# Stage-1 reads issued by ScalarE, and a later dispatch behind the gate, in an FFT convolution with mixture-of-experts and feed-forward kernel

## The chip, the cores and the metric

The kernel runs on one core of one Trainium2 chip. The metric is device microseconds of that core, median of 3 runs; lower is better. "us from the span's start" is the time axis of every row shown here.

## What is computed

The reference is a long convolution by FFT, a top-1 mixture of experts, and a dense layer pair with softplus between:

```python
y   = irfft(rfft(x, axis=1) * (filt_r + 1j * filt_i))        # x: 8 x 3072 x 256
x   = y.reshape(24576, 256)
e   = argmax(x @ w_gate, axis=1)                             # 8 experts, capacity 768 each
disp[e, pos] = x                                             # tokens in order, first 768 of an expert kept
out = gate_w * (relu(disp @ w1) @ w2)                        # 256 -> 1024 -> 256, back to its token
return softplus(out @ w_in) @ w_out                          # 256 -> 2048 -> 256
```

With these inputs the first three of the eight batches of 3072 tokens fill every expert's 768 places, so the main path convolves batches 0, 1 and 2 only; the rest of the output is one constant row. A check at the end branches to a general path when that does not hold; it is not taken here.

## The kernel before

**Stages.** The first quarter of the span is a pipeline that convolves three batches and dispatches their tokens; the rest is 16 units of 384 token slots, each with `w1`, `w2`, `wi`, `wo` (TensorE matmuls in split fp32r precision). The order of all work is written by hand: `ev(t, order, fn, ...)` puts a function into step `t`, and steps are emitted one after the other, within a step by `order`. This text counts steps from `c0`, the first of the pipeline, so "step 23" is `c0 + 23`. Each engine and each DMA queue runs its instructions in that order and stops at one whose semaphores are not there yet.

**Batches 1 and 2, first DFT.** `x1_out` (L213 to L222) writes the first stage's result to a DRAM tile `mid`; `load_i` (L224) reads a 128 x 2 x 256 piece `it` back in another layout, one for each of 12 columns `k`. The tile has four buffers. `s2` (L229) multiplies it (TensorE, L235) and filters it (VectorE, L239 to L242, and an add L243 on GpSimd for even `k`, on VectorE for odd `k`); `s3` (L247) is the next matmul, two steps after. Batch 1 has its `s2` in steps 18 to 29, batch 2 in steps 30 to 41. `tr2`, `s4` and `park` (L361) bring the tokens of a batch into the DRAM tile `parked`, by ScalarE copies and ScalarE's DMA queue.

**Gate and dispatch.** `gate` (L301) works out expert, slot and gate weight of a batch on VectorE in five steps. Then `marks` (L367) writes them from SP's queue: four DMAs of `ga` into `parked` (L372) and one of `ix` into the slot table `slots` (L373). `send` reads the table back (`load_index`, L390), `fetch` reads rows `lt` of one of eight groups (L394, three buffers), and `scatter` issues indirect DMAs `disp<-lt,ixt` of 128 rows (L398) on GpSimd, three to a group, 24 to a batch. `x_done` starts the loads `wst` of the dense weights (L452), which `convert` splits on VectorE, ScalarE and GpSimd from step 23 on, a new one every third step.

**The first unit.** `Unit.load_x` (L535) reads its rows `xd` from `disp` in step 50 once all scatters of batches 0 and 1 have landed; `gate_x` (L547) and `tr_x` (L555) follow, then `w1`. The loads `ws` of expert weights (L522) stand on the same SP queue.

**DMA semaphores.** A DMA of SP or ScalarE counts on one of eight semaphores, DMAHW0 to DMAHW7, which both queues use by turns; its issue waits until the DMA that last counted on the same one has landed.

Of the kernel before, what the change touches and what calls it, by code (L numbers as in the profile page):

```python
# [97 lines left out]
def body(tc, cap, x, ff, fx, wg, w1, w2, win, wout, m1, m2, m4, small, out):  # L98
    nc = tc.nc
    ctx = ExitStack()  # L100
    nunit = -(-cap // UNIT)
    lead = min(cap, UNIT)
# [14 lines left out]
    mid = [dram.tile([N1 * N2, D], F32, name=f"mid{b}") for b in range(1, STATIC)]  # L117
# [21 lines left out]
    class Conv:  # L139
# [84 lines left out]
        def load_i(self, b, k):  # L224

            self.it[b, k] = self.ip.tile([128, 2, D], F32, name="it", tag="it")
            nc.sync.dma_start(self.it[b, k], mid[b - 1].rearrange("(p k) c -> k p c", k=128)[:, 2 * k:2 * k + 2])

        def s2(self, b, k):  # L229

# [441 lines left out]
    with tc.manual_schedule():  # L672
        stl, stx, stf, stw, stm = (ExitStack() for _ in range(5))
        nc.scalar.preload_act_table_set(lnexp)
        cv = Conv(stl, stf, stx, "A")
# [54 lines left out]
        def ev(t, order, fn, *args):  # L730
            at.setdefault(t, []).append((order, len(at.get(t, ())), fn, args))
# [7 lines left out]
        T1, T2, S2, GG, S4, GATE, S3, X1, ON = range(-9, 0)  # L739
# [82 lines left out]
        c0, B = -72, (0, 17, 29)  # L822
        fills = cv.prefill()
        for b, s in enumerate(B):
            s += c0
            last = b == STATIC - 1
            for k in range(12):
                if b == 0:
                    if k % 2 == 0:
                        ev(s + k, T1 - 1, cv.make_m3, k // 2)  # L830
                    ev(s + k, T1, cv.tr1, b, k)
                else:
                    ev(s + k - 3, ON, cv.load_i, b, k)
                ev(s + k + 1, S2, cv.s2, b, k)
                ev(s + k + 3, S3, cv.s3, b, k)
            ev(s + 15, GG, cv.gsum, b)
            ev(s + 16, GG, cv.gturn, b)
            for k in range(5):
                ev(s + 17 + k, GATE, gate, b)
            for m in range(16):  # L840
                g, h = divmod(m, 2)
                t = s + 15 + (m // 2 if last else m * 13 // 16)
                ev(t, S4 + 0.5, cv.tr2, b, h, g)
                ev(t + 1, S4, cv.s4, b, h, g)
                if h:
                    ev(t + 1, ON, park, b, g)
            ev(s + 21, ON, cv.marks, b)
            if not last:
                ev(s + 21, ON, send, b, "lead")
                for _ in range(2):  # L850
                    ev(s + 21, ON, fetch)
        for g in range(8):
            ev(c0 + 5 + g, X1, cv.x1_out, 1, g)
            ev(c0 + 5 + g, ON, cv.load_x, 2, g)
            ev(c0 + 13 + g, X1, cv.x1_out, 2, g)
        for i in range(nslot // (4 * N1)):
            ev(c0 + 5 + i, ON, next, fills)
        for t in range(c0 + 22, -20):
            ev(t, ON, scatter, 2 if t < c0 + 46 else 3)
        ev(c0 + 22, ON, x_done)  # L860
        for t in range(c0 + 23, -24):
            ev(t, AHEAD - 0.5, convert, t < c0 + 45 and (t - c0) % 3 == 2)
# [7 lines left out]
        for v, u in enumerate(units):  # L870
            b = 16 * (v - 2)
# [9 lines left out]
            for i in range(KI):  # L881
                t = 16 * v + i
# [149 lines left out]
```

## Time and profile before

| | before |
|---|---|
| median of 3 runs | 1134.59 us (1133.48 to 1139.24) |
| profiled execution, its own time | 1130.57 us |
| span of its instructions | 1128.8 us |
| busy: TensorE matmul, VectorE, ScalarE, GpSimd | 92%, 42%, 71%, 53% of the span |
| mean granted TensorE clock | 0.967 of full speed |

The profiled execution is 4.0 us under the median of the runs, and 1.8 us of it lie outside the span. Busy shares are means over the convolution stages and the 16 units, which have different limits.

### The profile page before, as it was taken

What the parts mean: (1) busy time and instruction counts of PE and PEld (TensorE: products, weight loads), DVE (VectorE), ACT (ScalarE), POOL (GpSimd) and SP (SyncE); (2) the same over time, 40 slices, a digit from 0 to 9 for tenths busy, and PEclk for the clock granted to TensorE, in tenths of its full rate; (3) what the DMA queues carried; (4) which work ended last, traced back from release to release, by engine and by line L of the source; (5) the groups of instructions that cost most, each with busy time, mean ns of one, the idle gap of its engine ahead of it and who ended that gap; (6) DMA issues with size and microseconds to landing.
All of it is one profiled execution on the core that took longest, in us unless ns stands there. A gap on an engine that the chain in (4) does not pass through costs nothing.

```text
span 1128.8 us, 18362 instructions
## 1 busy us (share of the span) xinstructions
PE 1044.0 (92%) x6608; PEld 968.8 (86%) x6608; DVE 475.0 (42%) x929; ACT 804.8 (71%) x1690; POOL 598.2 (53%) x566
## 2 busy tenths in 40 slices
PE   9999688576778999999999999999999999999996
PEld 7756466345778999999999999999999999999996
DVE  3527599145877483323333333233332333332221
ACT  3555345265679888878788787888878788787885
POOL 0311470643646666677756565555656555654554
PEclk9999798786999999999999999999999999999999
DMA  9997884675543216643342323233211211100000
GB/s 311 322 299 227 236 261 82 201 234 151 153 128 104 68 54 226 225 142 110 105 135 96 130 90 132 93 116 109 67 61 53 61 53 56 58 10 15 15 15 18
DMA packets 111413, 141.67 MB, mean 126 GB/s; under 512 B 24366, under 2 KB 82987, under 8 KB 111312
## 3 DMA queue, kind: packets, MB, share of 16 engines
q1 hardware_dynamic: 94160, 112.02, 32.0%
q10 hardware_dynamic: 11392, 15.73, 4.8%
q0 software_dynamic: 5760, 12.65, 3.2%
q8 instruction: 54, 0.88, 0.3%
q14 instruction: 47, 0.39, 0.1%
HBM read 80.38 MB, written 63.15 MB: 127 GB/s over the span
## 4 chain that ended last, share of the span: by engine, by line
PE 70%; DVE 11%; DMA 6%; issue 5%; ACT 3%; POOL 3%; SPq 1%; ACTq 0%; POOLq 0%; DVEq 0%
PE pi L598 21%; PE po L621 21%; PE py L583 9%; PE pw L566 9%; PE p L219 2%; POOL gl L413 1%; DMA mid<-s 1%; PE p L199 1%; PE p L299 1%; DMA slots<-ix 1%; DMA wst<-in_win_dram 1%; DVE wrf L477 1%; DVE t L240 1%; DVE t L242 1%; DVE z L239 1%
## 5 line engine op out<-in xcount | busy, mean ns | idle before, releaser
L501 DVE SCALAR_TENSOR_TENSOR g<-pi,ln 128x384 f32<-128x384 f32 x256 | 142.8, 558 | 498.4 <-ACT ln L496 465.1
L413 POOL TENSOR_TENSOR gl<-g,gh 128x384 fp32r<-128x384 f32 x256 | 261.0, 1023 | 114.1 <-ACT gh L412 76.1
L621 PE MATMUL po<-woh,gh 128*128 128x256 f32 x768 | 214.9, 280 | 3.9 <-DVE ot L628 3.9
L621 PE MATMUL po<-woh,gl 128*128 128x256 f32 x768 | 215.6, 281 | 0.7 <-POOL gl L413 0.7
L621 PE MATMUL po<-wol,gh 128*128 128x256 f32 x768 | 215.8, 281 | 0.0
L493 ACT ACTIVATE ab<-pi 128x384 f32<-128x384 f32 x256 | 125.0, 488 | 114.4 <-PE pi L598 110.6
L598 PE MATMUL pi<-yh,wih 128*128 128x384 f32 x512 | 173.5, 339 | 6.4 <-DVE g L501 6.4
L598 PE MATMUL pi<-yl,wih 128*128 128x384 f32 x512 | 172.4, 337 | 0.0
L598 PE MATMUL pi<-yh,wil 128*128 128x384 f32 x512 | 172.1, 336 | 0.0
L413 POOL TENSOR_TENSOR w1l<-ws,w1h 128x512 fp32r<-128x512 f32 x64 | 83.6, 1306 | 136.2 <-ACT w1h L412 132.7
L621 PEld LDWEIGHTS po<-woh,gh 128*128 128x128 f32 x768 | 144.4, 188 | 4.7 <-DVE ot L628 2.8
L621 PEld LDWEIGHTS po<-woh,gl 128*128 128x128 f32 x768 | 144.8, 188 | 0.9 <-POOL gl L413 0.9
L621 PEld LDWEIGHTS po<-wol,gh 128*128 128x128 f32 x768 | 144.2, 188 | 0.0
L494 ACT ACTIVATE ab<-ab 128x384 f32<-128x384 f32 (+1 forms) x257 | 134.9, 525 | 8.2
L496 ACT ACTIVATE ln<-ab 128x384 f32<-128x384 f32 (+1 forms) x257 | 134.8, 524 | 8.1
L413 POOL TENSOR_TENSOR w2l<-ws,w2h 128x512 fp32r<-128x512 f32 x64 | 83.5, 1305 | 95.7 <-ACT w2h L412 94.0
L412 ACT CAST gh<-g 128x384 fp32r<-128x384 f32 x256 | 129.7, 507 | 0.3 <-DVE g L501 0.3
L598 PEld LDWEIGHTS pi<-yh,wih 128*128 128x128 f32 x512 | 96.4, 188 | 8.4 <-DVE g L501 8.4
L398 POOL DMA_INDIRECT disp<-lt,ixt x72 | 71.6, 994 | 54.4 <-DMA lt<-parked 38.9
L598 PEld LDWEIGHTS pi<-yl,wih 128*128 128x128 f32 x512 | 96.3, 188 | 0.0
L598 PEld LDWEIGHTS pi<-yh,wil 128*128 128x128 f32 x512 | 96.1, 188 | 0.0
L583 PE MATMUL py<-hh,w2h 128*128 128x384 f32 x256 | 90.0, 352 | 6.5 <-DVE yl L590 6.5
(132 smaller groups left out, 1965.6 us busy)
## 6 DMA issues: line engine op xcount, KB each, us to landing
ws<-in_w_dram SPq DMA_DIRECT2D x128, 256.0 KB, 2.8
out_dram<-cs SPq DMA_DIRECT2D x48, 512.0 KB, 3.9
lt<-parked SPq DMA_DIRECT2D x24, 387.0 KB, 4.7
xt<-in_x_dram SPq DMA_DIRECT2D x24, 384.0 KB, 8.0
parked<-yt ACTq DMA_DIRECT2D x24, 384.0 KB, 6.2
disp<-pf SPq DMA_DIRECT2D x16, 387.0 KB, 7.3
xd<-disp SPq DMA_DIRECT2D x48, 129.0 KB, 3.0
mid<-s ACTq DMA_DIRECT2D x16, 384.0 KB, 6.2
```

Source lines behind the costliest of these rows:

```text
L219: nc.tensor.matmul(ps.rearrange("q n c -> q (n c)"), lhsT=self.m1s, rhs=xt[:, 2 * i:2 * i + 2].rearrange("p n c -> p (n c)"), start=True, ...
L398: sc = nc.gpsimd.indirect_dma_start(out=disp[0:n], out_offset=bass.IndirectOffsetOnAxis(ap=index[b].bitcast(U32)[:, g, t:t + 1], axis=0), ...
L412: nc.scalar.copy(dst_hi, src)
L413: nc.gpsimd.tensor_tensor(out=dst_lo, in0=src, in1=dst_hi.bitcast(F32), op=ALU.subtract)
L493: nc.scalar.activation(out=ab[:, :n], in_=h, func=ACTF.Abs)
L494: nc.scalar.activation(out=ab[:, :n], in_=ab[:, :n], func=ACTF.Exp, scale=-1.0)
L496: nc.scalar.activation(out=ln[:, :n], in_=ab[:, :n], func=ACTF.Ln, bias=1.0)
L501: nc.vector.scalar_tensor_tensor(out=g[:, :n], in0=h, scalar=0.0, in1=ln[:, :n], op0=ALU.max, op1=ALU.add)
L566: nc.tensor.matmul(ps, lhsT=a[:, k, fs], rhs=b[:, k], start=(n == 0), stop=(n == 5))
L583: nc.tensor.matmul(self.py[d], lhsT=a[:, j % 2, ds], rhs=b, start=(j == 0 and n == 0), stop=(j == 7 and n == 2))
L598: nc.tensor.matmul(self.pi, lhsT=a[i][:, k], rhs=b[:, k], start=(n == 0), stop=(n == 5))
L621: nc.tensor.matmul(self.po[t], lhsT=a[:, ts], rhs=b[:, i], start=(i == 0 and n == 0), stop=(i == KI - 1 and n == 2))
```

## The change

Three things change, and nothing of what is computed. `load_i` issues its DMA from ScalarE's queue instead of SP's, and stands one step later (step `s + k - 2`). Behind a batch's gate, `marks` comes one step later, `send` with its two fetches two steps later. The scatters are in other steps: before, two to a step from step 22 on, and three from step 46 on, as long as there are any; now two to a step in steps 26 to 37 and three to a step in steps 43 to 50.

```diff
         def load_i(self, b, k):
...
-            nc.sync.dma_start(self.it[b, k], mid[b - 1].rearrange("(p k) c -> k p c", k=128)[:, 2 * k:2 * k + 2])
+            nc.scalar.dma_start(self.it[b, k], mid[b - 1].rearrange("(p k) c -> k p c", k=128)[:, 2 * k:2 * k + 2])
...
                 else:
-                    ev(s + k - 3, ON, cv.load_i, b, k)
+                    ev(s + k - 2, ON, cv.load_i, b, k)
...
-            ev(s + 21, ON, cv.marks, b)
+            ev(s + 22, ON, cv.marks, b)
             if not last:
-                ev(s + 21, ON, send, b, "lead")
+                ev(s + 23, ON, send, b, "lead")
                 for _ in range(2):
-                    ev(s + 21, ON, fetch)
+                    ev(s + 23, ON, fetch)
...
-        for t in range(c0 + 22, -20):
-            ev(t, ON, scatter, 2 if t < c0 + 46 else 3)
+        for t in range(26, 51):
+            if t < 38 or t > 42:
+                ev(c0 + t, ON, scatter, 2 if t < 38 else 3)
```

**SP's queue behind the gate of batch 0** (`parked_61` and `slots_64` are batch 0's, `mid_67` is batch 1's stage-1 result). Before, from the last prefill of `disp` on:

```order
L382 DMA disp<-pf 96x1032
L372 DMA parked_61<-ga 96x8x2 x4
L373 DMA slots_64<-ix 96x8x4
L390 DMA ixt<-slots_64 128x8x3
L394 DMA lt<-parked_61 128x774 x2
L227 DMA it<-mid_67 128x2x256 x2
L452 DMA wst<-in_win_dram 128x2x128 x4
L227 DMA it<-mid_67 128x2x256
```

The same place in the changed kernel, with the semaphores that each waits for:

```order
L372 DMA parked_61<-ga 96x8x2 [waits DMAHW1_49,DVE_49]
L372 DMA parked_61<-ga 96x8x2 [waits DMAHW2_49]
L372 DMA parked_61<-ga 96x8x2 [waits DMAHW3_49]
L372 DMA parked_61<-ga 96x8x2 [waits DMAHW5_49]
L373 DMA slots_64<-ix 96x8x4 [waits DMAHW6_49]
L452 DMA wst<-in_win_dram 128x2x128 [waits DMAHW7_49,DMAHW0_49,Activation_49]
L452 DMA wst<-in_win_dram 128x2x128 [waits DMAHW0_49,PE_49]
L452 DMA wst<-in_win_dram 128x2x128 [waits DMAHW2_49]
L452 DMA wst<-in_win_dram 128x2x128 [waits DMAHW3_49]
L390 DMA ixt<-slots_64 128x8x3 [waits DMAHW6_49,DMAHW4_49]
```

The loads of `wst` moved ahead of the read of the slot table, and no `it` is left on this queue.

**ScalarE, steps 22 to 24** in the changed kernel, from the load of step 22 to that of step 24 (`it` for columns 7, 8 and 9 of batch 1), with what each waits for:

```order
L227 DMA it<-mid_67 128x2x256 [waits DMAHW2_49,DMAHW1_49]
L300 COPY yt<-p_1059 96x4x128 [waits PE_49]
L265 COPY j<-p_1062 96x512 [waits PE_49]
L265 COPY j<-p_1069 96x512 [waits PE_49]
L256 COPY e<-p_1076 128x2x256 [waits PE_49]
L365 DMA parked_61<-yt 384x1x256 [waits DMAHW6_49,Activation_49]
L227 DMA it<-mid_67 128x2x256 [waits DMAHW0_49]
L300 COPY yt<-p_1107 96x4x128 [waits PE_49]
L300 COPY yt<-p_1110 96x4x128 [waits PE_49]
L265 COPY j<-p_1113 96x512 [waits PE_49]
L256 COPY e<-p_1120 128x2x256 [waits PE_49]
```

Before, the same copies and the park stand there without the two `it` rows. The semaphores tie these rows to SP's: DMAHW1 of the first row is that of SP's first mark, DMAHW6 of the park that of the slot table's write, DMAHW0 of the second `it` that of the second `wst`.

**GpSimd between the last adds of batch 2.** Before:

```order
L243 TENSOR_TENSOR z<-z,t_1689 128x512
L398 DMA disp<-lt,ixt 6144x258 x2
L488 TENSOR_TENSOR wil_1049<-wrf,wtop 128x256
L398 DMA disp<-lt,ixt 6144x258 x2
L243 TENSOR_TENSOR z<-z,t_1791 128x512
L398 DMA disp<-lt,ixt 6144x258 x4
```

Now:

```order
L398 DMA disp<-lt,ixt 6144x258 x4
L243 TENSOR_TENSOR z<-z,t_1687 128x512
L488 TENSOR_TENSOR wil_1035<-wrf,wtop 128x256
L243 TENSOR_TENSOR z<-z,t_1771 128x512
L488 TENSOR_TENSOR wil_1036<-wrf,wtop 128x256
L398 DMA disp<-lt,ixt 6144x258 x6
```

The last two adds now stand ahead of every scatter of batch 1.

## Rows read from the trace of the kernel before

**Rows 1.** Busy time by stretch: us, then each engine, clock, DMA share, GB/s.
```profile
126.00:186.00 60.00, 55.97 (x325) 41.72 (x323) 58.08 (x103) 29.68 (x58) 36.03 (x34) 0.94 0.73 223
360.00:1128.00 768.00, 752.46 (x5059) 749.71 (x5057) 260.00 (x511) 611.29 (x1294) 454.06 (x427) 1.00 0.26 85
```

**Rows 2.** TensorE in order of time: start, us, instruction [idle before <-releaser].
```profile
106.69 1.03 PE L235 MATMUL p<-it,m2s 128*128 128x256 f32 x4
...
124.81 2.05 PE L235 MATMUL p<-it,m2s 128*128 128x256 f32 x4 [10.54 <-DMA it<-mid]
...
130.46 1.03 PE L235 MATMUL p<-it,m2s 128*128 128x256 f32 x4
...
188.87 2.08 PE L235 MATMUL p<-it,m2s 128*128 128x256 f32 x4 [3.65 <-DVE t L242]
...
209.64 2.08 PE L254 MATMUL p<-m3s,z 128*128 128x128 f32 x8 [12.35 <-POOL z L243]
...
264.78 1.91 PE L555 MATMUL pt<-sm,xd 128*128 128x128 f32 x6 [10.31 <-ACT xd L547]
```

**Rows 3.** VectorE in order of time, the same columns.
```profile
126.19 0.29 DVE L473 TENSOR_SCALAR wtop<-wst 128x256 uint32<-128x256 uint32 x1 [13.50 <-DMA wst<-in_win_dram]
...
185.78 0.18 DVE L359 TENSOR_SCALAR tok<-tok 96x32 f32<-96x32 f32 x1
```

**Rows 4.** SP's DMA queue in order of time: start, us of issuing.
```profile
107.66 2.79 SPq L372 DMA_DIRECT2D parked<-ga  x4
110.48 0.54 SPq L373 DMA_DIRECT2D slots<-ix  x1
116.60 0.38 SPq L390 DMA_DIRECT2D ixt<-slots  x1
...
118.14 1.56 SPq L227 DMA_DIRECT2D it<-mid  x2
119.74 4.08 SPq L452 DMA_DIRECT2D wst<-in_win_dram  x4
...
185.77 2.06 SPq L372 DMA_DIRECT2D parked<-ga  x4
...
230.96 0.32 SPq L394 DMA_DIRECT2D lt<-parked  x1
...
253.72 2.07 SPq L372 DMA_DIRECT2D parked<-ga  x4
...
257.25 1.31 SPq L535 DMA_DIRECT2D xd<-disp  x3
```

**Rows 5.** GpSimd in order of time, the same columns as Rows 2.
```profile
202.81 1.01 POOL L398 DMA_INDIRECT disp<-lt,ixt  x1 [19.82 <-DMA lt<-parked]
...
238.72 0.97 POOL L398 DMA_INDIRECT disp<-lt,ixt  x1 [6.07 <-DMA lt<-parked]
...
241.94 0.97 POOL L398 DMA_INDIRECT disp<-lt,ixt  x1 [0.30 <-issue]
242.93 1.28 POOL L413 TENSOR_TENSOR w1l<-ws,w1h 128x512 fp32r<-128x512 f32 x1
```

**Rows 6.** ScalarE and its DMA queue in order of time.
```profile
238.03 0.56 ACTq L365 DMA_DIRECT2D parked<-yt  x1
238.63 0.40 ACT L489 CAST wih<-whb 128x256 fp32r<-128x256 f32 x1 [4.45 <-DMA lt<-parked]
...
264.21 1.31 ACT L547 ACTIVATE xd<-xd 128x256 f32<-128x256 f32 x3 [3.42 <-DMA xd<-disp]
```

**Rows 7.** DMA issues of 118 to 126 us: KB each, us to landing.
```profile
it<-mid SPq DMA_DIRECT2D x4, 256.0 KB, 6.2
```

**Rows 8.** DMA issues of the whole span, the same columns.
```profile
xd<-disp SPq DMA_DIRECT2D x48, 129.0 KB, 3.0
...
disp<-lt,ixt POOLq DMA_INDIRECT x72, 3.9
...
parked<-ga SPq DMA_DIRECT2D x12, 6.0 KB, 4.2
```

## The prediction

> **What bounds the kernel now.** I read the stretches first [rows 1]. From 360 us on TensorE is busy 752 of 768 us at full clock; the change touches nothing there, so all it can do lies ahead. There TensorE, in order of time, has three long stops [rows 2]: 10.54 us before step 25's `s2` at 124.81, 12.35 us before `s3` at 209.64, and 10.31 us before the first `tr_x` at 264.78. Between the first two, VectorE works 58.08 of 60 us [rows 1], so from 126 to 186 us VectorE sets the pace, and what reaches it earlier ends earlier. The reader is to see that the three stops hang on one queue, SP's.
>
> First stop: TensorE waits for `it`, and VectorE, 13.50 us, for the first `wst` [rows 2, 3]. Both are DMAs of SP, which at 107.66 issues the marks of batch 0, at 110.48 the slot table, and then stands until that has landed, at 116.60; the two `it` go out at 118.14 and `wst` at 119.74 [rows 4].
>
> Second stop: TensorE waits for GpSimd's add `z`, and that add stands behind scatters which waited 19.82 us for their rows, until 202.81 [rows 2, 5]. These rows come from the marks of batch 1, which went out at 185.77, as the gate's last instruction ended [rows 3, 4].
>
> Third stop: TensorE waits for ScalarE, ScalarE for `xd` at 264.21 [rows 2, 6]. `xd` was issued at 257.25, behind the marks of batch 2 at 253.72 on SP [rows 4], though GpSimd had issued the last scatter by 242.91 [rows 5].
>
> **The change part by part.** The sum is made against the profiled execution, 1130.57 us.
>
> *Loads off SP, `wst` ahead of the table's read.* On SP `wst` now follows the slot table's write, which was issued by 111.0. The first `wst` took 126.19 - 119.74 = 6.45 us from issue to VectorE [rows 3, 4], so VectorE can go on at 117.5 instead of 126.19: 8.7 us earlier. But `it` now stands on ScalarE, and shares semaphores with SP's DMAs. Column 7's load waits for the first mark: 107.66 plus 4.2 us of landing [rows 4, 8], 111.9, and lands 6.2 us later [rows 7], at 118.1. Behind it the park of step 23 waits for the slot table, 116.6, and column 8's load for the second `wst`, which I put 1 us after the first (four took 4.08 us to issue [rows 4]): 118.5. It lands at 124.7, and step 26's `s2`, at 130.46 before [rows 2], starts then: 5.8 us earlier. That is less than VectorE's 8.7, so the load sets it, and I take **-5.8 us**. Bounds: -8.7, if ScalarE's stops hide; 0, if the load is as late as before.
>
> From there VectorE's 58-of-60 stretch carries the shift to the end of gate 1: 185.78 becomes 180.0. The load has one step less to land in. Two steps took (124.81 - 10.54 - 106.69) = 7.6 us before the first stop [rows 2], a landing 6.2, so in steps 25 to 41 it mostly fits, with about 1 us over. The 24 issues cost ScalarE's queue some 0.4 us each (the DMA at 116.60 took 0.38 [rows 4]); ScalarE works 29.68 of 60 us there [rows 1], so they cost nothing as long as that stays idle, 24 x 0.4 = 9.6 us at worst.
>
> *Marks, `send` and scatters later.* The marks wait for the gate anyway, so a later step delays them by nothing: what releases them is VectorE's last write [rows 3, 4]. On GpSimd the last two adds of batch 2 now stand ahead of all scatters of batch 1, so the stop of 12.35 us goes. TensorE then reaches `s3` at 209.64 - 5.8 - 12.35 = 191.5, and needs, as before, 264.78 - 10.31 - 209.64 = 44.8 us from there to `tr_x` [rows 2]: ready at 236.3. What is late next is `xd`.
>
> *The chain to `xd`.* It no longer stands behind the marks of batch 2, but behind the last scatter. From marks to first scatter: 202.81 - 185.77 = 17.0 us [rows 4, 5]; the scatters' later steps (43 to 50) add nothing, because step 42, at 191.5, and one step of 3.9 us put TensorE past step 43 by then. From first to last scatter: 242.91 - 202.81 = 40.1 us [rows 5]. Of it GpSimd stood 6.07 us for the last group's rows, whose read was issued at 230.96 [rows 4, 5]; the tokens it reads are parked by ScalarE behind the second stop, so I let this wait go. One add leaves the stretch; two weight splits of 1.28 us [rows 5] come into it, with steps 48 and 49: +1.3, and as much again for waiting for ScalarE's half of a split, whose park can stand for a row read, as at 238.03 [rows 6]. That makes 36.6. The last scatter lands in 3.9 us, and `xd` in 3.0 by the median [rows 8] or 264.21 - 257.25 = 7.0 in this place [rows 4, 6]; I take 5.0, nearer to the middle because SP's neighbours there change. Sum 17.0 + 36.6 + 3.9 + 5.0 = 62.5 us, against 264.21 - 185.77 = 78.4: **-15.9 us**. Bounds: 17.0 + 34.0 + 3.9 + 3.0 = 57.9, or -20.5; 17.0 + 40.1 + 3.9 + 7.0 = 68.0, or -10.4. So `xd` is there at 242.5, after TensorE at 236.3: the third stop stays, about 6 us long, and the first unit starts 21.7 us earlier. The units behind it keep their order and lengths.
>
> **The sum.** -5.8 - 15.9 = -21.7 us: 1108.9 us for an execution like the profiled one. The median of the runs shown is 4.0 us above that execution, so on its scale I say **1113 us**. Bounds together: -8.7 - 20.5 = -29.2 and 0 - 10.4 = -10.4.
>
> **A rule against the change.** SP's queue held `it` for 10 us behind marks and table, with nothing of its own to wait for [rows 2, 4]. The Trainium skill, page "DMA: Bandwidth & Descriptors", section "Issuing engines are not separate DMA queues", says that DMAs started by different engines run on the same 16 DMA engines and interleave, and that spreading the issue only saves the sequencer's time to start them. By it the first term would be near zero, and the sum 1130.57 - 15.9 = 1114.7, or 1118.7 on the runs' scale. The trace disagrees on what an issuing queue is worth: what `it` lost there was a wait of its queue, not bandwidth.
>
> **The rivals.**
> *The loads are as late as before.* For it: on ScalarE they wait for the very marks, table and `wst` that held them on SP, and the estimate leaves only 5.8 us. Against: `wst` itself goes out 8.7 us earlier. Gain 15.9: 1118.7.
>
> *The first unit stays late.* ScalarE's parks wait for row reads, the reads for scatters, and the splits on GpSimd between the scatters for ScalarE behind its parks. For it: ScalarE stood 4.45 us at 238.63 for a row read [rows 6]. Three such waits inside the chain eat 13.4 of the 15.9: 1134.6 - 5.8 - 2.5 = 1126. Against: the splits come after 18 of 24 scatters, and the wait before was for the late last group.
>
> *Slower: a ring of waits on ScalarE in steps 28 to 38.* There `it` and parks share semaphores with the row reads of batch 0; a read waits for scatters about four steps back, a scatter stands on GpSimd behind adds for VectorE, VectorE behind TensorE, TensorE behind ScalarE. Four steps take 4 x (188.87 - 130.46) / 15 = 15.6 us now [rows 2]. The ring holds a scatter's 3.9, a read's 6 (taken as the load's 6.2 [rows 7]) and some 7 of GpSimd and VectorE lag, 17: nearly the same, and ScalarE can lag a step more unseen. It decides from 5.9 us a step on (21.7 us over 11 steps), a ring of 23.5; at 27 us the 11 steps lose 31 and the kernel takes 1144. The Trainium skill, "TensorE: Matmul & The Clock Gate", on engine queue depths, calls ScalarE a strict FIFO; a load that stands there stops every copy behind it, as the row at 238.63 shows.
>
> *Both terms at their better bounds:* -29.2, 1105.
>
> **How the numbers follow.** The forecast has 0.50, its own range 1108 to 1120; loads as late as before 0.20; first unit late 0.13; ring 0.10; both better 0.07. About 0.5%, 5.7 us, is what a measurement of this kernel can tell from no change. Faster: 0.50 + 0.20 + 0.07 and a part of the late first unit, 0.05: 0.82. Within it: the rest of that case and a mild ring, 0.09; slower 0.09. The range leaves out the ring and takes in the other cases up to the late first unit: 1105 to 1127.
>
> **What would show it.** In the profile after: `wst` on SP at about 111 and VectorE's first `wtop` near 117.5; the stop at step 25 split into short ones, step 26's `s2` near 124.7; the gate's last write of batch 1 near 180; no stop for `z`; first scatter of batch 1 near 197, last near 234, `xd` on ScalarE near 242.5, with `xd` ahead of the marks of batch 2. The prediction is wrong if TensorE waits for `it` by 1 us or more in most steps after 26, if GpSimd stops between scatters for more than 3 us in sum, or if the first `tr_x` starts later than 255.

## The result and the profile after

The changed kernel takes 1123.56 us, the median of 20 runs (1119.32 to 1135.12), beside 1138.51 us for 20 runs of the kernel before (1130.85 to 1143.59). The ratio is 0.9882, 95% interval 0.9861 to 0.9904: 13.4 us faster by the ratio, where 21.7 were forecast. The profiled execution is 1124.01 us with a span of 1122.1, which is 6.7 less than the span before. The profiled execution of before lay at the low end of its runs, which is why that pair is closer than the medians.

First the stretches, which answer to [rows 1]: us, busy time of each engine, granted clock, DMA share, GB/s.

```profile
126.00:186.00 60.00, 51.83 (x315) 38.31 (x314) 54.64 (x93) 29.51 (x58) 38.82 (x37) 0.99 0.78 237
...
360.00:1122.00 762.00, 747.07 (x5025) 744.67 (x5023) 254.21 (x502) 605.29 (x1280) 448.44 (x421) 1.00 0.26 86
```

From 360 us on nothing is different: TensorE works 98% of the stretch, as before. Between 126 and 186 us VectorE now works 54.64 of 60 us instead of 58.08: it waits where it did not wait before. TensorE of the changed kernel in order of time answers to [rows 2] (start, us, instruction, idle before it and its releaser):

```profile
88.22 1.13 PE L235 MATMUL p<-it,m2s 128*128 128x256 f32 x4 [2.13 <-DMA it<-mid]
...
123.78 2.04 PE L235 MATMUL p<-it,m2s 128*128 128x256 f32 x4 [3.54 <-DMA it<-mid]
131.44 1.10 PE L235 MATMUL p<-it,m2s 128*128 128x256 f32 x4 [2.78 <-DMA it<-mid]
...
195.19 1.06 PE L254 MATMUL p<-m3s,z 128*128 128x128 f32 x8
...
255.00 2.24 PE L555 MATMUL pt<-sm,xd 128*128 128x128 f32 x6 [4.77 <-ACT xd L547]
262.32 0.69 PE L566 MATMUL pw<-xh,w1h 128*128 128x384 f32 x1 [5.08 <-ACT xh L556]
```

The reader is to see three things. The stop of 10.54 us has become shorter ones for the same `it`, but step 26's `s2` starts at 131.44, no earlier than before. The stop of 12.35 us for `z` is gone: the `s3` that stood at 209.64 stands at 195.19. And the first unit, whose first `tr_x` comes 9.8 us earlier, then waits 5.08 us for `xh` where it waited 0.94, so that its first `pw` comes 5.3 us earlier, 262.32 against 267.63. The row of the kernel before for this last reading:

```profile
267.63 0.69 PE L566 MATMUL pw<-xh,w1h 128*128 128x384 f32 x1 [0.94 <-ACT xh L556]
```

The late first read, at 88.22, costs more than its own wait. After that stop TensorE's granted clock fell to 0.50, the lower of its two levels (1.2 GHz), in a stretch where it stood at 1.00 before (the kernel before first, then the changed one):

```profile
90.00:92.00 2.00, 2.00 (x12) 1.36 (x11) 1.92 (x5) 0.79 (x2) 0.00 (x0) 1.00 0.96 329
```

```profile
90.00:92.00 2.00, 2.00 (x7) 1.10 (x5) 1.91 (x5) 0.84 (x2) 0.34 (x1) 0.50 0.81 215
```

Step 18's `s2` is 3.0 us later than before (88.22 for 85.25), step 19's already 4.8 us (93.89 for 89.14). VectorE, which answers to [rows 3]:

```profile
122.00 0.29 DVE L473 TENSOR_SCALAR wtop<-wst 128x256 uint32<-128x256 uint32 x1 [5.41 <-DMA wst<-in_win_dram]
...
132.58 0.69 DVE L239 TENSOR_TENSOR z<-p,fr 128x512 f32<-128x512 f32 x1 [3.23 <-PE p L235]
...
186.71 0.18 DVE L359 TENSOR_SCALAR tok<-tok 96x32 f32<-96x32 f32 x1
```

VectorE gets its first `wst` 4.2 us earlier, but then waits for TensorE, which waits for `it`; gate 1 ends 0.9 us later than before. SP's queue, which answers to [rows 4]:

```profile
66.87 15.63 SPq L382 DMA_DIRECT2D disp<-pf  x9
...
111.55 2.06 SPq L372 DMA_DIRECT2D parked<-ga  x4
...
114.30 4.49 SPq L452 DMA_DIRECT2D wst<-in_win_dram  x4
...
186.70 2.05 SPq L372 DMA_DIRECT2D parked<-ga  x4
...
251.49 1.34 SPq L535 DMA_DIRECT2D xd<-disp  x3
252.93 2.64 SPq L372 DMA_DIRECT2D parked<-ga  x4
```

The marks of batch 0 now go out at 111.55, 3.9 us later than before. ScalarE and its queue, which answer to [rows 6]:

```profile
78.89 1.54 ACTq L227 DMA_DIRECT2D it<-mid  x1
...
85.58 1.89 ACTq L227 DMA_DIRECT2D it<-mid  x1
87.50 0.58 ACT L300 COPY yt<-p 96x512 f32<-96x512 f32 x1 [4.24 <-issue]
...
122.66 0.37 ACTq L227 DMA_DIRECT2D it<-mid  x1
123.06 1.07 ACT L300 COPY yt<-p 96x512 f32<-96x512 f32 x2 [5.19 <-DMA wst<-in_win_dram]
...
231.15 1.07 ACT L300 COPY yt<-p 96x512 f32<-96x512 f32 x2 [8.57 <-DMA ws<-in_w_dram]
...
238.94 0.62 ACT L412 CAST w1h<-ws 128x512 fp32r<-128x512 f32 x1
...
254.44 1.63 ACT L547 ACTIVATE xd<-xd 128x256 f32<-128x256 f32 x3 [1.74 <-DMA xd<-disp]
...
261.18 0.58 ACTq L365 DMA_DIRECT2D parked<-yt  x1
261.80 0.86 ACT L556 CAST xh<-pt 128x384 fp32r<-128x384 f32 x2 [4.77 <-DMA parked<-ga]
```

The copy at 87.50 has stood 4.24 us, in which ScalarE issued a park and a read of 1.89 us each. None of the copies at 123.06, 231.15 and 261.80 uses `wst`, `ws` or the marks. They stand behind a read or a park of ScalarE's own; in the built program eight completion semaphores go round over the DMAs of SP and ScalarE together, and each DMA waits for the one that had its semaphore before, on whichever of the two queues that was. The kernel before had such a stop too, for the marks of batch 2; it cost nothing there, since `xd` landed later still [rows 6]:

```profile
259.47 0.51 ACT L480 ACTIVATE whb<-wtop,ebias 128x256 uint32<-128x256 uint32 x1 [6.54 <-DMA parked<-ga]
```

GpSimd, which answers to [rows 5]:

```profile
203.66 1.01 POOL L398 DMA_INDIRECT disp<-lt,ixt  x1 [8.56 <-DMA lt<-parked]
...
226.83 0.97 POOL L398 DMA_INDIRECT disp<-lt,ixt  x1 [0.30 <-issue]
239.64 1.26 POOL L413 TENSOR_TENSOR w1l<-ws,w1h 128x512 fp32r<-128x512 f32 x1 [11.83 <-ACT w1h L412]
...
248.79 0.97 POOL L398 DMA_INDIRECT disp<-lt,ixt  x1 [0.30 <-issue]
```

After 18 of the 24 scatters GpSimd stands 11.83 us for ScalarE's half of a weight split. The chain of waits names the same three places, in order of time (start, us, what):

```profile
114.87 7.76 DMA wst<-in_win_dram
122.66 8.65 DMA it<-mid
...
228.99 10.61 issue
...
253.92 7.18 DMA parked<-ga
```

The times fit: a `wst` lands at 122.63 and ScalarE's read goes out at 122.66; the marks land at 261.10 and ScalarE's park goes out at 261.18.

### The profile page after: what moved, and what is told of

Same layout as the page of the kernel before. It is cut to its first block, busy times and chain, and to the rows that moved or that the text cites. A ratio compares the mean times of both kernels' runs of the same rounds, so it can differ in the third digit from the quotient of the medians.

```text
span 1122.1 us, 18349 instructions
## 1 busy us (share of the span) xinstructions
PE 1040.6 (93%) x6608; PEld 963.6 (86%) x6608; DVE 478.8 (43%) x929; ACT 804.6 (72%) x1690; POOL 598.1 (53%) x566
## 4 chain that ended last, share of the span: by engine, by line
PE 71%; DMA 8%; DVE 6%; issue 6%; ACT 3%; POOL 3%; SPq 1%; POOLq 0%; ACTq 0%; DVEq 0%
PE pi L598 22%; PE po L621 22%; PE py L583 9%; PE pw L566 9%; DMA it<-mid 2%; DMA mid<-s 2%; PE p L235 2%; POOL disp L398 1%; PE p L199 1%; PE p L219 1%; PE p L299 1%; POOL gl L413 1%; PE p L254 1%; DVE wr L475 1%; DMA xt<-in_x_dram 1%
## 5 line engine op out<-in xcount | busy, mean ns | idle before, releaser
L243 POOL TENSOR_TENSOR z<-z,t 128x512 f32<-128x512 f32 x24 | 31.0, 1292 | 126.1 <-DVE t L242 94.9
```

The costliest lines, as they stand in the source:

```text
L243: (nc.vector if b > 0 and k % 2 else nc.gpsimd).tensor_tensor(out=z, in0=z, in1=t2, op=ALU.add)
```

## The experiments

The theory after this trace: the later marks, `send` and scatters made the gain, and issuing the reads on ScalarE took part of it back, since they wait there for semaphores of SP's transfers and stand behind ScalarE's copies. The main rival: the moved reads do help, and the loss lies elsewhere, in the scatters' chain. Further rivals stand with each run.

The table has every run's profiled execution and its comparison: marks of batch 0 and batch 1 on SP, last scatter of batch 1, first `pw`, the span less that `pw` (all us), the median, and the ratio to before on the same chip with its interval. Runs 1 to 4 shared one chip and runs 5 to 12 another; the kernel before has 1133.24 us beside runs 1 to 4, 1140.16 beside 5 to 8 and 1139.61 beside 9 to 12.

| run | marks 0 | marks 1 | last scatter | first `pw` | span less `pw` | median | ratio |
|---|---|---|---|---|---|---|---|
| before | 107.66 | 185.77 | 241.94 | 267.63 | 861.2 | 1138.51 | |
| after | 111.55 | 186.70 | 248.79 | 262.32 | 859.8 | 1123.56 | 0.9882 (0.9861 to 0.9904) |
| 1 loads only | 112.50 | 188.79 | 249.30 | 272.84 | 862.8 | 1135.71 | 1.0011 (0.9991 to 1.0031) |
| 2 moves only | 108.14 | 180.29 | 239.03 | 251.38 | 861.6 | 1114.75 | 0.9824 (0.98 to 0.9849) |
| 3 four a step | 113.06 | 186.83 | 241.57 | 259.78 | 859.6 | 1121.50 | 0.9886 (0.9855 to 0.9916) |
| 4 moves, four | 107.31 | 178.59 | 229.05 | 247.93 | 860.7 | 1112.28 | 0.9815 (0.9778 to 0.9852) |
| 5 old step | 113.50 | 184.41 | 248.47 | 262.03 | 862.0 | 1124.95 | 0.9863 (0.9832 to 0.9895) |
| 6 prefills too | 115.94 | 194.54 | 257.24 | 271.27 | 861.8 | 1133.21 | 0.9936 (0.9914 to 0.9958) |
| 7 moves, parks | 108.37 | 180.36 | 239.09 | 246.64 | 867.0 | 1114.64 | 0.9779 (0.9746 to 0.9811) |
| 8 all four edits | 108.05 | 179.81 | 234.28 | 246.89 | 866.6 | 1115.17 | 0.9783 (0.9752 to 0.9814) |
| 9 after again | 113.87 | 192.52 | 255.28 | 269.59 | 861.9 | 1130.53 | 0.9902 (0.987 to 0.9934) |
| 10 moves again | 106.90 | 179.24 | 241.55 | 256.77 | 861.5 | 1120.21 | 0.9817 (0.9786 to 0.9847) |
| 11 moves, four, `xd` | 108.60 | 180.91 | 234.19 | 254.85 | 860.6 | 1116.66 | 0.9785 (0.9753 to 0.9817) |
| 12 moves, four again | 106.70 | 179.81 | 232.36 | 252.22 | 862.2 | 1114.86 | 0.9779 (0.975 to 0.9808) |

Except in runs 7 and 8 the span less the first `pw` is the same to 3.2 us, 859.6 to 862.8. So the first `pw` is what to watch, as the prediction took it, and what differs by more lies ahead of it.

Whatever else was changed, the marks of batch 0 go out at 106.70 to 108.60 in the eight profiles with the reads on SP, and at 111.55 to 115.94 in the six with the reads on ScalarE. With the later `send`, the marks of batch 1 go out at 178.59 to 180.91 with the reads on SP (seven profiles) and at 184.41 to 194.54 with them on ScalarE (five).

**1. The reads' move alone.** The kernel before with

```
-            nc.sync.dma_start(self.it[b, k], mid[b - 1]...
+            nc.scalar.dma_start(self.it[b, k], mid[b - 1]...
-                    ev(s + k - 3, ON, cv.load_i, b, k)
+                    ev(s + k - 2, ON, cv.load_i, b, k)
```

> The kernel before, with only the reads of stage 1 moved to ScalarE and one step later; marks, send and scatters stay. Theory (the loads' move gained nothing by itself): without the reads between them SP issues the prefills in one burst (nine in 15.6 us after the change, against some 30 us before), the first reads come late, step 18's s2 is near 88 instead of 85.3, the marks of batch 0 near 111 instead of 107.7, and ScalarE's reads wait for semaphores of SP's transfers. Gate 1's marks then go out at 186 or later, the stop for z stays at about 12 us, and the time is that of before, ratio 0.997 to 1.004. Rival (the prediction's first term, eaten only by the moved steps): gate 1's marks at 180 and 5.8 us gained, ratio 0.995.

Ratio 1.0011: no gain. Gate 1's marks come at 188.79, not at 180, and the stop for `z` stays. One row of SP and one of TensorE of this run:

```profile
67.78 14.68 SPq L382 DMA_DIRECT2D disp<-pf  x9
```

```profile
212.62 2.08 PE L254 MATMUL p<-m3s,z 128*128 128x128 f32 x8 [13.53 <-POOL z L243]
```

And SP of the kernel before, in the place of the first:

```profile
74.01 0.39 SPq L227 DMA_DIRECT2D it<-mid  x1
74.47 0.46 SPq L382 DMA_DIRECT2D disp<-pf  x1
74.97 0.42 SPq L227 DMA_DIRECT2D it<-mid  x1
```

Before, reads and prefills took turns; with the reads on ScalarE, SP writes nine prefills in a row and the marks of batch 0 come 4.8 us later.

**2. The other moves alone.** The changed kernel with the two lines above set back to SP and `s + k - 3`.

> The changed kernel with the reads of stage 1 back on SP at their old step; marks, send and scatters are later as in the change. Theory: the whole gain is in these moves, and the reads' move to ScalarE ate some of it. Marks of batch 0 are back near 107.7, the first wst goes out near 112 instead of 114.3, gate 1's marks near 181 to 183 instead of 186.7, no stop for z, and the time is 3 to 6 us below the changed kernel: ratio to before 0.983 to 0.986. Rival: SP's queue blocks the reads again behind the table's read and the row reads, 10 us at step 25 as before, so that gate 1's marks come at 186 or later and the ratio is 0.990 or above.

Ratio 0.9824, a little more gain than the theory's 0.983 to 0.986. Gate 1's marks come at 180.29, though the reads are on SP and share its queue with the table and the row reads. VectorE and SP of this run:

```profile
120.24 0.29 DVE L473 TENSOR_SCALAR wtop<-wst 128x256 uint32<-128x256 uint32 x1 [7.06 <-DMA wst<-in_win_dram]
```

```profile
180.29 2.06 SPq L372 DMA_DIRECT2D parked<-ga  x4
```

From VectorE's first `wtop` to these marks are 60.1 us; before, 185.77 - 126.19 = 59.6 [rows 3, 4]; in the changed kernel 64.7. With the reads on SP the stretch keeps its length and starts earlier, since `send` no longer stands ahead of `wst`. With the reads on ScalarE it starts earlier too, and loses 5.1 us on the way. No run has the later `send` without the later scatters, or the reverse; which of them gives what is read from the rows and not tested.

**5 and 6. What the reads do on ScalarE.** Run 5 is the changed kernel with the reads one step earlier (`s + k - 3`, on ScalarE); run 6 the changed kernel with

```
-                nc.sync.dma_start(dv[a], pf)
+                nc.scalar.dma_start(dv[a], pf)
```

> The changed kernel with the reads of stage 1 on ScalarE, but at their old step, one earlier. Theory (the reads are late because they are issued on ScalarE, behind its copies, parks and their semaphores, while SP writes its prefills in a burst): the lead of one more step gives back a part, step 18's s2 between 85.5 and 87.5 and the marks of batch 0 between 108 and 110.5; gate 1's marks stay between 183 and 187; ratio to before 0.985 to 0.990. Rival (it is the one step less in which to land): marks of batch 0 at 107.7 and gate 1's at 180 to 181, ratio 0.981 to 0.984, as with the reads on SP.

> The changed kernel with the sixteen prefills of the dispatch table issued by ScalarE too, so that they stand between the reads as they did on SP before. Theory (SP's burst of prefills makes the first reads late): step 18's s2 back at 85.3 to 86.5, marks of batch 0 at 107.5 to 109, gate 1's marks 3 us earlier than the changed kernel's 186.7, ratio 0.984 to 0.988. Rival (ScalarE's own queue makes them late): s2 of step 18 at 88 or later, since ScalarE now issues still more, marks of batch 0 at 111 or later, ratio 0.988 or above.

Both expectations take it that the reads are late. In these two runs step 18's `s2` does not wait for `it`; it starts at 87.89 and 87.66, still over 2 us later than before, and behind it TensorE stops for ScalarE's copies. Run 5, then run 6:

```profile
91.07 1.99 PE L299 MATMUL p<-j,m4s 96*96 96x512 f32 x2 [2.15 <-ACT j L265]
```

```profile
99.06 1.10 PE L219 MATMUL p<-xt,m1s 96*96 96x512 f32 x2 [2.70 <-ACT j L265]
```

The copies are late because ScalarE is issuing: in run 5 a park of 1.52 us and a read of 2.68 us go out from 85.67 on, and the next copy, at 89.95, has stood 4.66 us. The marks of batch 0 come at 113.50 and 115.94. So with a step more of lead (run 5) the first reads are there in time and batch 0 is as late as ever: the reads' issues on ScalarE are enough to make it late, by its copies where not by the reads. Run 5's `s2` and marks lie outside what the theory gave; its gate 1's marks come 2.3 us earlier than in the changed kernel, and the ratio, 0.9863, lies in the theory's range.

Run 6 goes against the part on the prefills: they no longer stand in a row on SP, and the marks are later still. As they then stood in ScalarE's queue too, the run does not say what the burst costs by itself; that stays open. The DMA share does not settle it: from 76 to 88 us it is 0.97 in the changed kernel, but also 0.99 in the kernel before, where reads and prefills took turns (0.71 in run 6); only from 66 to 76 us is it higher with the burst, 1.02 by the profile's count beside 0.82.

**3 and 4. The scatters ahead of the splits.** Run 3 is the changed kernel with the following, run 4 the same with the reads on SP.

```
-            if t < 38 or t > 42:
-                ev(c0 + t, ON, scatter, 2 if t < 38 else 3)
+            if t < 38 or 42 < t < 49:
+                ev(c0 + t, ON, scatter, 2 if t < 38 else 4)
```

> The changed kernel with four scatters a step in steps 43 to 48 instead of three in 43 to 50, so that all 24 stand ahead of the weight splits on GpSimd. Theory (the 11.83 us that GpSimd stood for ScalarE's half of a split, behind parks, is what the second term lost): GpSimd does not stop for w1h between scatters, the last scatter comes near 240 instead of 249.8, xd on ScalarE near 245, and the time is 6 to 10 us below the changed kernel: ratio to before 0.980 to 0.983. Rival (the last group's rows are as late, since ScalarE's parks are): the last scatter waits for rows instead and stays within 3 us of 249.8; the ratio is that of the changed kernel, 0.986 to 0.990.

> Both: reads on SP at their old step, later marks, send and scatters, and four scatters a step. If the two causes add, the ratio to before is 0.977 to 0.980 and the last scatter comes near 235; if only the one for the splits counts, that of the run with four scatters alone, 0.980 to 0.983; if neither, 0.986 to 0.990.

In run 3 the last scatter comes 7.2 us earlier, as the theory says, but the time is the changed kernel's, as the rival says, and for a reason that neither had. On SP, weight loads that wait for buffers of the same splits now stand ahead of `xd`, which goes out at 248.55, 7.0 us after the last scatter starts. But that is not what ends last: ScalarE takes `xd` without a wait for it, and the chain of waits ends elsewhere (ScalarE of run 3, then its chain):

```profile
255.64 1.30 ACT L547 ACTIVATE xd<-xd 128x256 f32<-128x256 f32 x3
```

```profile
253.77 4.80 DMA parked<-ga
258.65 0.56 ACTq L365
```

Ahead of `xh` stands a park, and the park waits for the marks of batch 2, which batch 2's gate released at 252.81 and which the first unit does not use. The chains of runs 4, 11 and 12 come to the first `pw` by the same marks and park. (Earlier in run 3's chain stand 8.39 and 3.47 us for which the profile names no queue.) In run 4 the marks of batch 0 and 1 are early as in run 2, the last scatter is at 229.05, and the ratio is 0.9815, short of the sum of both (in run 12 the same kernel has 0.9779, within it).

**11. `xd` ahead of those loads.** Run 4 with

```
-            ev(b - 16 if v > 2 else (-22, -20, -11)[v], AHEAD,
+            ev(b - 16 if v > 2 else (-24, -20, -11)[v], AHEAD if v else ON,
```

> Reads on SP, later moves, four scatters a step, and the read of the first unit's rows ahead of the weight loads in SP's program (parks stay on ScalarE). Theory (with four scatters xd stood on SP behind weight loads that wait for splits, some 7 us after the last scatter): xd is issued within 4 us of the last scatter, TensorE's stop for it falls from 2.6 us to under 1, first pw near 246, 1 to 3 us below four scatters alone. Rival (the weight loads that now stand behind xd are late instead): the stop moves into the first unit, and the time is that of four scatters alone or longer.

`xd` is issued 3.8 us after the last scatter starts, and the stop for it is 1.01 us, about as the theory has it; but the first `pw` comes at 254.85, and the median is 1.8 us above run 12, whose runs it overlaps. That agrees with run 3, where `xd` was not what ended last. TensorE of run 11, then of run 12:

```profile
220.72 3.73 PE L299 MATMUL p<-j,m4s 96*96 96x512 f32 x4 [12.39 <-ACT j L265]
...
245.01 3.73 PE L299 MATMUL p<-j,m4s 96*96 96x512 f32 x4 [4.52 <-ACT j L265]
...
254.85 0.69 PE L566 MATMUL pw<-xh,w1h 128*128 128x384 f32 x1 [3.18 <-ACT xh L556]
```

```profile
219.94 3.73 PE L299 MATMUL p<-j,m4s 96*96 96x512 f32 x4 [11.70 <-ACT yt L300]
```

TensorE is late behind ScalarE. The first stop stands in both runs; the one of 4.52 us has no counterpart in run 12. What holds ScalarE at the first of them is again a park, in run 11 one that waits for a row read:

```profile
218.42 0.51 ACT L480 ACTIVATE whb<-wtop,ebias 128x256 uint32<-128x256 uint32 x1 [12.92 <-DMA lt<-parked]
```

**7 and 8. The parks off ScalarE.** Run 7 is run 2 with the following; run 8 has run 4's and run 11's edits as well.

```
-            nc.scalar.dma_start(rows, self.yt[b, g][:, :, 0:D])
+            (nc.sync if b == STATIC - 1 else nc.scalar).dma_start(rows, self.yt[b, g][:, :, 0:D])
```

> Reads on SP, later marks, send and scatters, and the parks of batch 2 issued by SP instead of ScalarE. Theory (ScalarE's half of the first split is late since ScalarE stands with a park that waits for an earlier transfer of SP on the same completion semaphore): ScalarE's stops of 6.81 and 5.80 us at 213 and 222 and GpSimd's stop of 8.19 us for w1h shrink to under 3 us each, xh does not wait for marks, the first pw starts 5 to 9 us earlier than 251.4, and the time falls by as much against the kernel with ScalarE's parks: ratio to before 0.974 to 0.978. Rival (the split is late because its weights are, which SP loads behind row reads that wait for scatters): GpSimd's stop stays at 6 us or more and the ratio at 0.981 to 0.985.

> All that helped: reads on SP, later marks, send and scatters, four scatters a step, parks of batch 2 on SP, and the read of the first unit's rows ahead of the weight loads that wait for splits. Theory (each was a queue's wait in the chain to the first unit): the last scatter at 228 to 232, xd on SP within 5 us behind it, TensorE's stop for xd under 2 us, first pw at 243 to 246, ratio to before 0.974 to 0.979. Rival (TensorE itself is ready no earlier than 242 to 245): no better than four scatters with reads on SP, ratio 0.979 to 0.983.

In run 7 GpSimd no longer stands for `w1h` between scatters, and `xh` does not wait for marks: the first `pw` comes at 246.64 with 0.21 us of waiting, 4.7 us earlier than in run 2. The theory holds for the place of these waits. But the last scatter is no earlier than in run 2 (239.09 and 239.03), since GpSimd now stands for rows between scatters, 5.26 us at 231.42 the longest time. And TensorE then stops inside the first unit, for VectorE, which stands for a dense weight (TensorE, then VectorE):

```profile
246.64 0.69 PE L566 MATMUL pw<-xh,w1h 128*128 128x384 f32 x1 [0.21 <-ACT xh L556]
...
263.02 0.69 PE L583 MATMUL py<-hl,w2h 128*128 128x384 f32 x1 [4.16 <-DVE hl L571]
```

```profile
261.54 0.29 DVE L473 TENSOR_SCALAR wtop<-wst 128x256 uint32<-128x256 uint32 x1 [5.32 <-DMA wst<-in_win_dram]
```

The span less `pw` is 867.0 in run 7 and 866.6 in run 8 instead of 861.6, so some 5 us are given back. That the weight came late behind SP's parks is likely from SP's order, but was not tested. What run 7 gains on the whole is not settled. Its span is that of run 2, which ran on another chip (1113.6 and 1113.0), and 4.7 us less than that of run 10, the same kernel as run 2 on run 7's chip (1118.3); the intervals of runs 7 and 10 overlap. Run 8 is equal to run 7 (1115.17 and 1114.64), so no gain of run 4's and run 11's edits shows there.

**9, 10 and 12. Side by side.** The changed kernel, run 2 and run 4 again on one chip, with run 11.

> The changed kernel again, on the same chip as the next three, so that they can be compared with it directly. Ratio to before 0.986 to 0.990 as before; marks of batch 1 at 186 to 188 and first pw near 262.

> Reads on SP at their old step, later marks, send and scatters, again. Theory (the reads' move to ScalarE costs 6 to 11 us of what the other moves give): 6 to 11 us below the changed kernel on the same chip, marks of batch 1 near 180, first pw near 251. Rival (the two earlier ratios differ because of the chips): within 3 us of the changed kernel.

> Reads on SP, later moves and four scatters a step, again, beside the others on one chip. Theory: 1 to 4 us below reads on SP with three scatters a step, as in the first comparison. Rival (it only moves the wait from GpSimd to SP's queue): equal to it within 1 us.

Reads on SP are 10.3 us below the changed kernel, 1120.21 against 1130.53, and no run of the one lies among those of the other (1117.39 to 1120.92; 1125.82 to 1133.31). Four scatters a step give another 5.4 us, 1114.86 (1113.83 to 1116.91), more than was expected; the first comparison gave 2.5, with runs that overlap. That version, reads on SP, later marks, `send` and scatters, four scatters a step, has 0.9815 and 0.9779, ahead of both kernels; runs 7, 8 and 11 (0.9779 to 0.9785) cannot be told from it. The changed kernel missed what was expected of it here: ratio 0.9902, marks of batch 1 at 192.52, first `pw` at 269.59. A further `it` was late (TensorE waited 4.16 us for it at 153.66). Run 10's first `pw`, 256.77, is 5.8 us later than expected.

## Why the prediction was right in sign and too large

The sum was right in direction, and the range of 1105 to 1127 held the time, but 1123.56 lies outside the likeliest case's own 1108 to 1120. That case did not come. What came was the first rival, loads as late as before, and a part of the second, the first unit late, both at once, which the prediction had priced only one by one; the range held because of its rivals and not because of its sum. Of -21.7 us the profiled pair shows -5.3 at the first `pw`, and three terms make that difference, +6.7, +5.2 and +4.5. (The 13.4 us between the medians are more, and cannot be split in this way from one profile of each.)

- **The first term, -5.8, is the step that failed.** It said that column 8's read sets gate 1, goes out at 118.5 and lets step 26's `s2` start at 124.7. It went out at 122.66, 4.2 us later, of which 3.3 us are `wst` at 114.30 instead of 111.0, behind the later marks of batch 0; and it landed 8.65 us later instead of 6.2, with the DMA engines full as they were at this place before (the profile counts a share of 1.09 from 122.66 to 131.30 us, and 1.04 from 118 to 126 before; no run says what of this is transfer and what is queue). So `s2` came at 131.44, gate 1's marks at 186.70 instead of 180.0, and the term was +0.9 instead of -5.8. The text counted an issue of ScalarE at 0.4 us and took the issues as free. It did not look at steps 15 to 18, where the first read now goes out at 78.89 instead of 74.01, issues take up to 1.89 us, ScalarE's copies stand behind them (runs 5 and 6), and SP runs its prefills ahead, at a cost that stays open. The gate's end at 180 was reached in run 2, by another part of the change: `send` two steps later puts `wst` ahead of the table's read, and the reads had better stay on SP.
- **A rule on the reads.** By the Trainium skill, page "DMA: Bandwidth & Descriptors", section "Issuing engines are not separate DMA queues", starting DMAs from several engines saves only the sequencer's time to start them. The prediction held the trace against that rule. Run 1 agrees with the rule (1.0011), and runs 9 and 10 show more than it says: the move cost 10.3 us. ScalarE's rows show how: what an issuing engine stands for, its other work stands for too (4.24 and 5.19 us behind moved reads; 8.57 and 4.77 us behind parks, which stood on ScalarE before).
- **The stop for `z`** is gone as said; the `s3` behind it came 14.5 us earlier.
- **The chain to `xd`, -15.9, came to -10.7.** From marks to first scatter: 17.0, as said. From first to last scatter: 46.1 instead of 36.6, for the 1.3 us "for waiting for ScalarE's half of a split" were 11.83. This is the mechanism of the rival that the first unit stays late, with one long wait in place of three short ones. The rest, from the last scatter to `xd` on ScalarE, was 4.7 instead of 8.9.
- **`xd` ahead of the marks of batch 2** was right (251.49 and 252.93), but the first `pw` also needs `xh`, and ScalarE's park ahead of it waited for those marks: 7.3 us from `tr_x` to `pw` instead of 2.85, +4.5. No step of the prediction looked behind `xd`, though ScalarE had stood 6.54 us for these marks before the change, at 259.47.
- **The ring on ScalarE** did not come: in the changed kernel's profile no `s2` of steps 27 to 40 waits more than 1.61 us for anything; in run 9 one of them waited 4.16 us for `it`. Of the three signs that would make the prediction wrong, GpSimd's stop of over 3 us between scatters came, and the first `tr_x` stood at the bound of 255.

## What to carry to other kernels

In this kernel a DMA put on a computing engine waited in that engine's order, for its turn and for the completion semaphore that it reuses, and every copy behind it waited too; before moving one, list for each such DMA which earlier transfer it reuses the semaphore of, and when that lands. When reads and prefills shared SP's queue they took turns; relieved of the reads, SP ran ahead with the prefills: ask what it will issue in the time that it gains. And where a chain has several queues' waits in a row, taking one away mostly uncovers the next (behind the scatters the marks of batch 2 in run 3, behind ScalarE's parks a late weight in run 7), so measure the end of the chain and not the wait.

## What the runs showed that was not expected

The same kernel differs by several us between profiled executions, and all of it ahead of the first `pw`: the changed kernel had it at 262.32 and 269.59 with spans of 1122.1 and 1131.5, run 2 and run 10 at 251.38 and 256.77 with 1113.0 and 1118.3, while the rest took 861.6 and 861.5 us in the latter two. Run 2 and run 10 ran on different chips, so the two causes, chip and execution, are not told apart. The part of this kernel that waits for transfers varies; the part bound by TensorE hardly does.
